# Top-k attention and a gated layer on one core: a layer's rows cast and transposed by DMAs, the sums' constant added by a product, one reduction for row maximum and threshold

## The chip, the cores and the metric

The kernel runs on one core of a Trainium2 chip. The core has five engines with a queue each: TensorE (PE, with its weight loads PEld), VectorE (DVE), ScalarE (ACT), GpSimd (POOL) and SyncE (SP), which here only issues DMAs. An engine works its own queue in order and waits for the others through semaphores. The metric is the device time of one execution in microseconds; before the change it is 821.52 us in the median of three runs.

## The reference

Attention over 8 batches and 8 heads, 576 rows of 64 elements each, in which a row keeps only its 32 largest scores, and behind it a gated (highway) layer of 512 columns over all 4608 rows.

```python
scores = scale * np.matmul(q, k.transpose(0, 1, 3, 2))
kth = np.partition(scores, -top_k, axis=-1)[..., -top_k:-top_k + 1]
mask = scores >= kth
scores = np.where(mask, scores, -1000000000.0)
scores = scores - np.max(scores, axis=-1, keepdims=True)
attn = np.exp(scores)
attn = attn / (np.sum(attn, axis=-1, keepdims=True) + 1e-09)
out = np.matmul(attn, v)
# the heads side by side are x, 4608 x 512
H = np.maximum(x @ w_h, 0.0)
T = 1.0 / (1.0 + np.exp(-(x @ w_t + b_t)))
return T * H + (1.0 - T) * x
```

## The kernel before

The work is cut into units of 128 query rows of one head. A batch has 576 = 4 x 128 + 64 rows, so it has 32 full units, and four units more that each hold the last 64 rows of two heads. Two units make a pair, 18 pairs make a batch, 144 pairs the whole. The main loop, `step(i)`, runs once for every pair, and is a software pipeline: in step i the pair i+2 gets its scores, pair i+1 its threshold, pair i its exponentials and counts, pair i-1 its masks, and pair i-3 its product with v. The order of the instructions on each engine is the order in which `step` writes them (`tc.manual_schedule`); nothing is reordered later.

**One pair's way.** `scores` multiplies q and k in fp32 on TensorE into a PSUM tile of three banks (L293, L302; L310 and L319 for the short units). On VectorE twelve `max` instructions take the eight largest of each sixth of a row (`segments`, L337, into `cand`). `refine` (L342 to L368) merges these lists and ends in a threshold that stands for about the 24th largest score: the list `mid` (L363), and its maximum, written to `wall[:, u, 0]` (L367). `row_max` (L372) reduces the first column of `cand` to the row's maximum in `tk`. `biases` (L375) multiplies both on GpSimd into the biases that ScalarE uses.

ScalarE copies the scores to SBUF (`copy_scores`, L332), then marks and counts the scores above the threshold with a sign pass (`mask_count`, L381). TensorE adds those marks to the PSUM tile (`mask_add`, L394), so that the marked scores sink, and VectorE's `below` (L404) takes the eight largest of what is left. From the count, `hits`, `pick_a` and `pick_b` (L410, L420, L423) choose the exact 32nd value. ScalarE computes the exponentials (`expo`, L400) and a step (`above`, L427), or GpSimd computes the step (`above_one`, L438). VectorE multiplies the exponentials by it (`keep_min`, `keep_mul`, L434, L444), a DMA transposes the product on SP's queue (`transposes`, L465), and `values` (L478) multiplies it with v on TensorE: five products per head accumulate into one PSUM bank, 65 columns each. The 65th column of the v tile `vb` is a constant, 1.0, so that this column of the result is the row's sum.

**The layer.** When a block of 128 rows has all its heads, ScalarE copies the bank to SBUF (`xs_copy`, L492), and `norm` (L538) takes over: VectorE adds 1e-9 to the sum and doubles it (L541), inverts it (L542), and GpSimd multiplies the rows by it (L547). Three pieces follow, one for each step: `xt` transposes the fp32 rows on TensorE (L560) and ScalarE copies them to bf16 (L564); `hh` and `tt` are the two projections (`project`, L506) with their ReLU and tanh on ScalarE (L575, L597). The pieces wait in `ready`, then `layers`, and `late` holds the copy that belongs to the piece of the step before. The sums behind them run on GpSimd and as an accumulating DMA (L658).

**Fillers.** `spare` (L262) issues products whose result nobody reads, on columns of the value bank that are otherwise free: 8 in each step, and 4 more if the step has a layer piece, or 10 more if it has none. The next batch's k and q are loaded by SP, v by GpSimd (`loads_v`, L174, one DMA per head), and `prep_filler` transposes k and q on TensorE (L239), one piece in a step, from the step `k_in` = 6 of a batch on.

Of the kernel before, what the change touches and what calls it, by code (L numbers as in the profile page):

```python
# [10 lines left out]
ALU = mybir.AluOpType  # L11
FP32 = mybir.dt.float32
# [5 lines left out]
J = 4  # L18
# [8 lines left out]
def kernel(  # L27
# [69 lines left out]

    wall = consts.tile([P, NU, NPK], FP32)
    fac = consts.tile([P, 4], FP32)
    nc.vector.memset(fac[:, 0:2], -scale)  # L100
    nc.vector.memset(fac[:, 2:4], -BIGK * (1.0 - 2.0**-24))
    tk = consts.tile([P, NG + 1, 4], FP32)
    be = consts.tile([P, NG + 1, 4], FP32)
    NE = 4
# [5 lines left out]
    csum = consts.tile([P, NU], FP32)  # L110
    nc.vector.memset(tk[:, 0, 2:4], 0.0)
    nc.vector.memset(tk[:, NG, 0:2], 0.0)

    def top(u):
        return tk[:, u // 2, u % 2 : u % 2 + 1]

    def kth(u):
        return tk[:, u // 2 + 1, 2 + u % 2 : 3 + u % 2]

    def tb(u):  # L120
        return be[:, u // 2, u % 2 : u % 2 + 1]

    def eb(u):
        return be[:, u // 2 + 1, 2 + u % 2 : 3 + u % 2]

    NM = 4
    masks = []
# [44 lines left out]
    def loads_v(b, vb):  # L172
        def head(h):
            nc.gpsimd.dma_start(  # L174
                vb[:, h, 0:J, 0:D],
                v[b, h, 0 : J * P, :].rearrange("(p j) d -> p j d", j=J),
            )
# [6 lines left out]
        return [partial(head, h) for h in range(H)] + [partial(ends, o) for o in (0, P2)]  # L184

# [156 lines left out]
    def refine(g, cand):  # L342
        u0, u1 = pairs[g][0], pairs[g][1] + 1
        en = ends[g % NE]
        runs = cand[:].rearrange("p s (k t) r -> p (s k) t r", t=2)
        one, two = runs[:, :, 0, :], runs[:, :, 1, ::-1]
# [3 lines left out]
        mid = cpool.tile([P, 2, 8], FP32, name="mid")  # L350
        nc.vector.tensor_tensor(high[:].rearrange("p (k r) -> p k r", r=8), one, two, ALU.max)  # L351
        yield
        nc.vector.tensor_tensor(low[:].rearrange("p (k r) -> p k r", r=8), one, two, ALU.min)
# [12 lines left out]
        yield  # L366
        nc.vector.tensor_reduce(wall[:, u0:u1, 0], mid[:], mybir.AxisListType.X, ALU.max)  # L367
        yield  # L368


    def row_max(g):
        nc.vector.tensor_reduce(tk[:, g, 0:2], st[g]["cand"][:, :, :, 0], mybir.AxisListType.X, ALU.max)  # L372

    def biases(g):
        return nc.gpsimd.tensor_tensor(be[:, g, :], tk[:, g, :], fac[:], ALU.mult)  # L375

    def mask_count(u, ps):
        m1 = masks[u % NM]  # L380
        nc.scalar.activation(  # L381
            m1[:].bitcast(I8)[:, 1 : 2 * S : 2],
            ps,
            AF.Sign,
            bias=wall[:, u, 0:1],
            scale=ABOVE,
            accum_out=csum[:, u : u + 1],
        )
        return m1
# [13 lines left out]
    def below(u, ps):  # L403
        nc.vector.max(wall[:, u, 1:NPK], ps)  # L404

# [12 lines left out]
    def pick_a(pair, hit):  # L418
        u0, u1 = pair[0], pair[1] + 1
        nc.gpsimd.tensor_tensor(hit[:], hit[:], wall[:, u0:u1, :], ALU.mult)  # L420

    def pick_b(pair, hit):
        nc.vector.tensor_reduce(tk[:, pair[0] // 2 + 1, 2:4], hit[:], mybir.AxisListType.X, ALU.add)  # L423

# [108 lines left out]
    def ffn_pieces(b, qt, xs):  # L533
# [4 lines left out]
        def norm():  # L538
            xs3 = xs[:, 0 : nh * DE].rearrange("p (h e) -> p h e", e=DE)
            rinv = cpool.tile([P, H], FP32, name="rinv")  # L540
            nc.vector.tensor_scalar(rinv[:, 0:nh], xs3[:, :, D], 1e-9, 2.0, ALU.add, ALU.mult)  # L541
# [62 lines left out]
    def blk_norm(k):  # L604
# [3 lines left out]
        rinv = cpool.tile([P, H], FP32, name="rinv")  # L608
        nc.vector.tensor_scalar(rinv[:, 0:nh], xs3[:, :, D], 1e-9, 2.0, ALU.add, ALU.mult)
        nc.vector.reciprocal(rinv[:, 0:nh], rinv[:, 0:nh])  # L610
        nc.vector.tensor_tensor(
# [32 lines left out]

    adds, stores = [], []

# [40 lines left out]
    def start_scores(g):  # L687
# [5 lines left out]
        st[g]["seg"] = 0  # L693
        st[g]["cand"] = cpool.tile([P, 2, NSEG, 8], FP32, name="cand")

# [42 lines left out]
    def step(i):  # L738
# [7 lines left out]
        if live and b + 1 < B:  # L746
# [15 lines left out]
        if prev:  # L762
            pu, ps_ = pairs[i - 1], st[i - 1]
            ps_["r"] = [above(pu[0], ps_["sc"][0])]
            ps_["r"].append(above_one(pu[1], ps_["sc"][1]) if len(pool_work) < (3 if last_steps else 5) else None)
        if late:
            late.pop(0)()
# [25 lines left out]
        ra = refine(i + 1, st[i + 1]["cand"]) if nxt else iter(())  # L793
        for _ in range(2):
            next(ra, None)
        if live:
            hit = hits(pr)
            pick_a(pr, hit)
        added = bool(adds)
        if adds:  # L800
            do_add(i)
        elif todo_v:
# [12 lines left out]
        for _ in ra:  # L815
            pass
        last = None
        for s in range(2):
            if prev:
                u = pu[s]  # L820
                if ps_["r"][s] is not None:
                    ep, last = (keep_min, keep_mul)[s](u, ps_["e"][s], ps_["r"][s])
                else:
                    ep, last = keep(u, ps_["sc"][s], ps_["e"][s])
                ps_["et"][s] = transposes(ep)
        if live:
# [3 lines left out]
        if nxt:  # L830
            masks_of(i + 1)
        while stores and stores[0][0] <= i:
            stores.pop(0)[1]()
# [3 lines left out]
    def begin():  # L837
# [22 lines left out]
        for _ in refine(0, st[0]["cand"]):  # L860
            pass
        row_max(0)
        biases(0)
# [18 lines left out]
    def sure(j, src, scale):  # L882

        nc.scalar.activation(
            signs[:].rearrange("p (g t) -> p g t", t=2),
            src,
# [6 lines left out]
    def finish():  # L893
# [51 lines left out]
        old["et"][0] = transposes(ep)  # L945
        nc.vector.tensor_tensor(hit[:], hit[:], wall[:, pr[0] : pr[1] + 1, :], ALU.mult)
        pick_b(pr, hit)
# [3 lines left out]
        for s, home in enumerate((bank(x2, 1), bank(x1, 0))):  # L951
# [4 lines left out]
            nc.scalar.copy(cur["et"][s][:].rearrange("p c q -> p (c q)"), turned)  # L956
        sure(0, tk[:, 1 : NG + 1, 2:4], 1.0)
        sure(1, tk[:, 0:NG, 0:2], -1.0)
        values_of(i - 1, 0)
# [5 lines left out]
        do_work(nc.vector, NG * dm)  # L965
        nc.vector.scalar_tensor_tensor(cond[:], wall[:, :, 1], ABOVE, wall[:, :, 0], ALU.mult, ALU.add)
        while stores:
            stores.pop(0)[1]()
        sure(2, cond[:].rearrange("p (g t) -> p g t", t=2), 1.0)
        blk_norm(yb)  # L970
# [117 lines left out]
```

## Time and profile before

| | |
|---|---|
| median of three runs | 821.52 us (821.15 to 821.84) |
| the profiled execution | 822.81 us |
| its span, first to last instruction | 821.2 us |
| mean granted TensorE clock | 0.996 |
| one batch of 18 steps, steady | 98.6 us |
| DMA data moved | 91.61 MB |

The profile's page gives each engine's busy time and its share of the span; the chain of work that ended last, followed back from the last instruction; the groups of instructions by source line, with number, busy time, mean duration of one in ns and the idle time of the engine ahead of them; and the DMA queues. The waits are listed by who waited for whom, with the total in us, the number of times and the longest. The windows give the busy time of each engine in a stretch of the span, and the timeline the instructions in order, as start, duration, engine, line. Instructions on one engine overlap: the next can start before the one in front has ended, so the distance of two starts is what an instruction costs its engine, and its duration is longer.

### The profile page before, as it was taken

What the parts mean: (1) busy time and instruction counts of PE and PEld (TensorE: products, weight loads), DVE (VectorE), ACT (ScalarE), POOL (GpSimd) and SP (SyncE); (2) the same over time, 40 slices, a digit from 0 to 9 for tenths busy, and PEclk for the clock granted to TensorE, in tenths of its full rate; (3) what the DMA queues carried; (4) which work ended last, traced back from release to release, by engine and by line L of the source; (5) the groups of instructions that cost most, each with busy time, mean ns of one, the idle gap of its engine ahead of it and who ended that gap; (6) DMA issues with size and microseconds to landing.
All of it is one profiled execution on the core that took longest, in us unless ns stands there. A gap on an engine that the chain in (4) does not pass through costs nothing.

```text
span 821.2 us, 21236 instructions
## 1 busy us (share of the span) xinstructions
PE 714.2 (87%) x6687; PEld 517.6 (63%) x6687; DVE 784.9 (96%) x4162; ACT 772.7 (94%) x1438; POOL 556.1 (68%) x703
## 2 busy tenths in 40 slices
PE   7888988898889988889898898888988898888884
PEld 5666666666666666666666666666666666666552
DVE  6999999999999999999999999999999999999985
ACT  5999999999999999999999999999999999999983
POOL 2666777776677776777667776777667767666550
PEclk9999999999999999999999999999999999999998
DMA  6698878885568655775567765777556865444462
GB/s 120 84 137 140 109 105 129 140 118 84 107 126 142 108 91 110 131 137 108 83 121 132 137 104 72 133 139 131 92 94 129 142 113 97 92 88 72 103 90 74
DMA packets 323145, 91.61 MB, mean 112 GB/s; under 512 B 312144, under 2 KB 315216, under 8 KB 323024
## 3 DMA queue, kind: packets, MB, share of 16 engines
q1 hardware_dynamic: 272688, 74.76, 46.3%
q0 software_dynamic: 48656, 14.95, 18.5%
q8 instruction: 55, 0.90, 0.5%
q10 hardware_dynamic: 1680, 0.46, 0.3%
q14 instruction: 66, 0.54, 0.2%
HBM read 31.72 MB, written 9.44 MB: 50 GB/s over the span
## 4 chain that ended last, share of the span: by engine, by line
DVE 43%; ACT 39%; PE 13%; issue 2%; DMA 1%; SPq 0%; DVEq 0%; ACTq 0%
DVE cand L337 16%; DVE wall L404 12%; ACT m L381 11%; ACT e L400 8%; ACT sc L332 7%; ACT r L427 5%; PE xs L310 4%; PE pso L262 3%; DVE ep L434 3%; DVE ep L444 2%; ACT kT L240 2%; PE xs L293 1%; ACT xs L492 1%; ACT qT L240 1%; DVE en L358 1%
## 5 line engine op out<-in xcount | busy, mean ns | idle before, releaser
L337 DVE MAX8 cand<-xs 128x8 f32<-128x96 f32 x1728 | 297.4, 249 | 13.9 <-PE xs L319 9.4
L262 PE MATMUL pso<-cst,ident_b 128*128 128x252 bf16 x1935 | 256.5, 272 | 38.8 <-ACT xs L492 36.7
L438 POOL TENSOR_SCALAR ro<-sc,tk 128x576 bf16<-128x576 f32 x136 | 234.8, 1726 | 0.0
L262 PEld LDWEIGHTS <-ident_b 128*128 128x128 bf16 x1935 | 183.4, 98 | 77.8 <-issue 45.9
L400 ACT ACTIVATE e<-sc,be 128x576 bf16<-128x576 f32 x288 | 228.6, 794 | 0.0
L404 DVE MAX8 wall<-xs 128x8 f32<-128x576 f32 x288 | 204.3, 751 | 4.2 <-PE xs L394 3.6
L293 PE MATMUL xs<-kT,qT 64*128 64x256 f32 x1024 | 145.6, 400 | 35.2 <-DVE high L351 28.8
L332 ACT COPY sc<-xs 128x1152 f32<-128x1152 f32 x144 | 162.1, 1126 | 1.5 <-DVE cand L337 1.3
L293 PEld LDWEIGHTS xs<-kT,qT 64*128 64x128 f32 x1024 | 93.6, 186 | 64.7 <-issue 32.4
L381 ACT ACTIVATE m<-xs,wall 128x576 int8<-128x576 f32 x144 | 108.5, 754 | 13.1 <-DVE wall L367 10.7
L420 POOL TENSOR_TENSOR hit<-hit,wall 128x18 f32<-128x18 f32 x143 | 32.1, 225 | 128.4 <-DVE hit L410 119.1
L394 PE MATMUL xs<-m,ident_b 128*128 128x512 bf16 (+1 forms) x576 | 104.2, 285 | 11.9 <-ACT m L381 9.2
L381 ACT ACTIVATE m<-sc,wall 128x576 int8<-128x576 f32 x144 | 113.0, 784 | 0.0
L427 ACT ACTIVATE r<-sc,be 128x576 bf16<-128x576 f32 x143 | 111.4, 779 | 0.0
L375 POOL TENSOR_TENSOR be<-tk,fac 128x4 f32<-128x4 f32 x144 | 28.9, 201 | 93.4 <-DVE ep L444 51.8
L478 PEld LDWEIGHTS <-et 128*128 128x128 bf16 (+1 forms) x1600 | 68.6, 100 | 21.0 <-issue 3.5
L478 PE MATMUL pso<-vb,et 128*128 128x65 bf16 (+1 forms) x1600 | 74.6, 194 | 1.7 <-DMA et<-ep 1.6
L394 PEld LDWEIGHTS <-ident_b 128*128 128x128 bf16 x576 | 50.7, 97 | 39.7 <-issue 18.3
L302 PEld LDWEIGHTS xs<-kd,qT 128*128 128x128 f32 x256 | 38.1, 188 | 42.5 <-issue 42.1
L434 DVE TENSOR_TENSOR ep<-e,r 128x576 bf16<-128x576 bf16 x143 | 64.6, 452 | 0.1
L302 PE MATMUL xs<-kd,qT 128*128 128x128 f32 x256 | 62.5, 326 | 0.0
L444 DVE TENSOR_TENSOR ep<-e,ro 128x576 bf16<-128x576 bf16 x136 | 61.4, 452 | 0.0
(130 smaller groups left out, 1107.7 us busy)
## 6 DMA issues: line engine op xcount, KB each, us to landing
kin<-in_k_dram SPq DMA_DIRECT2D x64, 128.0 KB, 2.9
qin<-in_q_dram SPq DMA_DIRECT2D x62, 128.0 KB, 3.0
out_dram<-s SPq DMA_DIRECT2D x30, 256.0 KB, 2.5
s<-h POOLq DMA_DIRECT2D x29, 256.0 KB, 4.1
vb<-in_v_dram POOLq DMA_DIRECT2D x80, 64.0 KB, 3.2
et<-ep SPq DMA_TRANSPOSE x286, 2.7
kin<-in_k_dram SPq DMA_DIRECT2D x16, 64.0 KB, 2.4
qin<-in_q_dram SPq DMA_DIRECT2D x14, 64.0 KB, 2.5
```

Source lines behind the costliest of these rows:

```text
L262: nc.tensor.matmul(po["t"][:, 4 * DE : BANK], ident_b[:], cst[:, 0 : BANK - 4 * DE], start=True, stop=True, skip_group_check=True,)
L293: nc.tensor.matmul(ps[:, mo + n0 : mo + n0 + 256], qT[r : r + D, hp, qs : qs + P], kT[r : r + D, hp, n0 : n0 + 256], start=(n0 == 0), stop ...
L302: nc.tensor.matmul(ends, qT[:, hp, qs : qs + P], kd[:, hp, :], start=True, stop=True)
L332: nc.scalar.copy(sc[:], both)
L337: nc.vector.max(cand[:, s, :], sc[:, s * SEG : (s + 1) * SEG])
L381: nc.scalar.activation(m1[:].bitcast(I8)[:, 1 : 2 * S : 2], ps, AF.Sign, bias=wall[:, u, 0:1], scale=ABOVE, accum_out=csum[:, u : u + 1],)
L394: nc.tensor.matmul(ps[:, s0:s1], ident_b[:], m1[:, s0:s1], start=False, stop=True, skip_group_check=True)
L400: nc.scalar.activation(e[:], sc, AF.Exp, bias=tb(u), scale=scale)
L404: nc.vector.max(wall[:, u, 1:NPK], ps)
L427: nc.scalar.activation(r[:], sc, AF.Relu, bias=eb(u), scale=BIGK)
L438: nc.gpsimd.tensor_scalar(r[:], sc, kth(u), None, ALU.is_ge)
L478: nc.tensor.matmul(pso[r0 : r0 + ql, col : col + DE], ets[s][:, c, gi * P2 : gi * P2 + ql], vb[:, h, vc, :], start=(c == 0), stop=(c == nc ...
```

## The change

- `column` loads v for batches 1 to 7 in four DMAs, each with a quarter of the rows of all eight heads, in place of eight DMAs of one head each.
- The constant column of `vb` is 2.0, and `values` opens each head's chain with one more product: a row of ones (1 x 128, or 1 x 64) by a row `tiny` that is zero except for 2e-9 in its last column, both fp32. The bank's last column is then twice the sum, plus 2e-9, and `norm` and `blk_norm` only invert it.
- `refine` writes its list `mid` into the second column of `cand` (which now has eight lists in place of six, two of them padded with -3e38), and one reduction takes the maximum of the first and the second column, that is, the row maximum and the threshold, into neighbouring columns of `wall`. `row_max` and `tk` are gone; `wall` holds their values.
- The first of the two masks (`masked(0)`) is issued between the writing of the list and that reduction; `pick_b` moves in front of the list.
- For 37 of the 40 blocks, `cast` (a DMA from GpSimd's queue, fp32 to bf16, SBUF to SBUF) and two steps later `turn` (a transposing DMA on SP's queue) take the place of `xt`. Casts are issued where no accumulating DMA is due in the step, ahead of the loads of v.
- Preparation of the next batch starts at `k_in` = 4 in place of 6. It is skipped in a step that has a layer's copy waiting, unless it would come late, and a layer piece is issued during the preparation only in a step that prepares.

```diff
-        nc.gpsimd.memset(vb[:, :, :, D:DE], 1.0)
+        nc.gpsimd.memset(vb[:, :, :, D:DE], 2.0)
+    tiny = consts.tile([1, DE], FP32)
+    nc.vector.memset(tiny[:], 0.0)
+    nc.vector.memset(tiny[:, D:DE], 2.0e-9)
+    row1 = consts.tile([1, P], FP32)
+    nc.vector.memset(row1[:], 1.0)
...
+        def column(j):
+            nc.gpsimd.dma_start(
+                vb[:, :, j, 0:D],
+                v[b, :, 0 : J * P, :].rearrange("h (p j) d -> p h j d", j=J)[:, :, j, :],
+            )
+        mains = [partial(column, j) for j in range(J)] if b else [partial(head, h) for h in range(H)]
...
         nc.vector.scalar_tensor_tensor(
-            out=mid[:], in0=en[:, 1, :, 0:8], scalar=-1.0, in1=en[:, 0, :, 0:8], op0=ALU.mult, op1=ALU.min
+            out=cand[:, :, :, 1], in0=en[:, 1, :, 0:8], scalar=-1.0, in1=en[:, 0, :, 0:8], op0=ALU.mult, op1=ALU.min
         )
         yield
-        nc.vector.tensor_reduce(wall[:, u0:u1, 0], mid[:], mybir.AxisListType.X, ALU.max)
+        nc.vector.tensor_reduce(
+            wall[:, u0:u1, TOP : THR + 1],
+            cand[:, :, :, 0:2].rearrange("p s r k -> p s k r"),
+            mybir.AxisListType.X,
+            ALU.max,
+        )
-    def row_max(g):
-        nc.vector.tensor_reduce(tk[:, g, 0:2], st[g]["cand"][:, :, :, 0], mybir.AxisListType.X, ALU.max)
...
             for gi, h in enumerate(heads):
+                nc.tensor.matmul(
+                    pso[r0 : r0 + ql, col : col + DE], row1[:, 0:ql], tiny[:], start=True, stop=False
+                )
                 for c in range(nck):
...
-                        start=(c == 0),
+                        start=False,
...
-            nc.vector.tensor_scalar(rinv[:, 0:nh], xs3[:, :, D], 1e-9, 2.0, ALU.add, ALU.mult)
-            nc.vector.reciprocal(rinv[:, 0:nh], rinv[:, 0:nh])
+            nc.vector.reciprocal(rinv[:, 0:nh], xs3[:, :, D])
...
-                ready.extend([xt, hh, tt])
+                if by_dma:
+                    casts.append(cast)
+                else:
+                    ready.extend([xt, hh, tt])
+        by_dma = isinstance(b, int) and units[-1][0:2] > (b, qt + 2)
+        def cast():
+            xb = xpool.tile([P, dm], BF16, name="xb")
+            nc.gpsimd.dma_start(xb[:, 0:w], st["x"][:, 0:w])
+            return partial(turn, xb)
+        def turn(xb):
+            st["xT"] = fpool.tile([P, n_g, P], BF16, name="xT")
+            nc.sync.dma_start_transpose(st["xT"][:, 0:ng, :], xb[:, 0:w])
+            ready.extend([hh, tt])
...
-            if k_in == (6 if b else 7):
+            if k_in == (4 if b else 7):
...
-        ev = prep_filler()
+        ev = None if busy and i > SPB and len(to_prep) < 16 - k_in else prep_filler()
...
-        if layers:
+        if layers and (not to_prep or ev or last_steps):
             late.append(layers.pop(0)())
...
-        if nxt:
-            row_max(i + 1)
-        next(ra, None)
         if live:
             pick_b(pr, hit)
+        next(ra, None)
+        masked(0)
         for _ in ra:
             pass
+        last = masked(1)
```

More of the change, by code (lines that the diff above doesn't have):

```diff
@@ L96 @@
         nc.vector.memset(pidx[:, jj : jj + 1], S - 2.0 * (TOP_K - jj))
[L98 to L103, printed above, removed]
+    TOP, THR, KTH = 0, 1, NPK + 1
+    wall = consts.tile([P, NU + 2, NPK + 2], FP32)
+    fac = consts.tile([P, 2, 2], FP32)
+    nc.vector.memset(fac[:, :, 0], -scale)
+    nc.vector.memset(fac[:, :, 1], -BIGK * (1.0 - 2.0**-24))
+    be = consts.tile([P, NG + 1, 2, 2], FP32)
     NE = 4
@@ L110 @@
     csum = consts.tile([P, NU], FP32)
[L111 to L115, printed above, removed]
+    nc.vector.memset(wall[:, 0:2, KTH : KTH + 1], 0.0)
     def kth(u):
-        return tk[:, u // 2 + 1, 2 + u % 2 : 3 + u % 2]
+        return wall[:, u + 2, KTH : KTH + 1]
     def tb(u):
-        return be[:, u // 2, u % 2 : u % 2 + 1]
+        return be[:, u // 2, u % 2, 0:1]
     def eb(u):
-        return be[:, u // 2 + 1, 2 + u % 2 : 3 + u % 2]
+        return be[:, u // 2 + 1, u % 2, 1:2]
+    cands = []
+    for i in range(4):
+        cand = consts.tile([P, 2, 8, 8], FP32, name=f"cand{i}")
+        nc.vector.memset(cand[:, :, NSEG:, 0:1], -3.0e38)
+        cands.append(cand)
     NM = 4
@@ L344, in refine @@
         en = ends[g % NE]
-        runs = cand[:].rearrange("p s (k t) r -> p (s k) t r", t=2)
-        one, two = runs[:, :, 0, :], runs[:, :, 1, ::-1]
+        one = cand[:, :, 0:NSEG:2, :]
+        two = cand[:, :, 1:NSEG:2, ::-1]
         high = cpool.tile([P, 2 * HALF], FP32, name="high")
@@ L643, in blk_out @@
         return k["b"], k["qt"], o
-    adds, stores = [], []
+    adds, stores, casts, turns = [], [], [], []
     def do_work(engine, width):
@@ L765, in step @@
             ps_["r"].append(above_one(pu[1], ps_["sc"][1]) if len(pool_work) < (3 if last_steps else 5) else None)
+        busy = bool(late)
         if late:
@@ L793, in step, with masked @@
         ra = refine(i + 1, st[i + 1]["cand"]) if nxt else iter(())
+        def masked(s):
+            if not prev:
+                return None
+            u = pu[s]
+            if ps_["r"][s] is not None:
+                ep, ins = (keep_min, keep_mul)[s](u, ps_["e"][s], ps_["r"][s])
+            else:
+                ep, ins = keep(u, ps_["sc"][s], ps_["e"][s])
+            ps_["et"][s] = transposes(ep)
+            return ins
         for _ in range(2):
@@ L798, in step @@
             pick_a(pr, hit)
-        added = bool(adds)
+        added = bool(adds or casts)
         if adds:
             do_add(i)
+        elif casts:
+            turns.append((i + 2, casts.pop(0)()))
         elif todo_v:
@@ L831, in step @@
             masks_of(i + 1)
+        while turns and turns[0][0] <= i:
+            turns.pop(0)[1]()
         while stores and stores[0][0] <= i:
@@ L861, in begin @@
             pass
-        row_max(0)
         biases(0)
```

43 lines of the change are left out of this document (16 added, 27 removed).

## The prediction

> **What bounds the kernel now.** I read the page's busy times and its chain first, then the waits, then one steady batch (18 steps) in the windows, then the timeline of two steps.
>
> ```profile
> span 821.2 us, 21236 instructions
> PE 714.2 (87%) x6687; PEld 517.6 (63%) x6687; DVE 784.9 (96%) x4162; ACT 772.7 (94%) x1438; POOL 556.1 (68%) x703
> DVE 43%; ACT 39%; PE 13%; issue 2%; DMA 1%; SPq 0%; DVEq 0%; ACTq 0%
> ...
> 403.09:501.67 98.58, 87.65 (x827) 63.64 (x826) 96.06 (x515) 96.03 (x180) 70.65 (x89) 1.00 0.64 116
> ```
>
> DVE and ACT are both full: of a batch's 98.58 us they work 96.06 and 96.03. PE comes third with 87.65, and the chain already runs through it for 13%. So the reader should not see one bound but three, two at 97% and one at 89%. What PE does with the other 107.0 us (821.2 less 714.2) is in the waits:
>
> ```profile
> PE pso L262 <- ACT xs L492: 36.7, 70, 0.8
> PE xs L293 <- DVE high L351: 28.8, 48, 1.5
> PE xs L394 <- ACT m L381: 9.2, 33, 0.6
> PE xs L310 <- DVE high L351: 6.0, 7, 0.9
> PE xs L293 <- DVE wall L404: 3.7, 16, 0.4
> ```
>
> The first row is no slack. PE finishes the value products, ACT copies the bank, and only then may the filler products (`spare`) write the same bank again; the timeline shows that wait at its shortest:
>
> ```profile
> 409.62 0.48 PE L478 MATMUL pso<-vb,et 128*128 128x65 bf16 x10
> 410.14 0.38 ACT L492 COPY xs<-pso 128x260 f32<-128x260 f32 x1 [0.16 <-PE pso L478]
> 410.57 1.02 PE L262 MATMUL pso<-cst,ident_b 128*128 128x252 bf16 x8 [0.46 <-ACT xs L492]
> ```
>
> ACT starts 0.04 us after the products end (409.62 + 0.48 = 410.10) and PE still loses 0.46. Seventy times 0.46 are 32 us that stay whatever ACT does. The other four rows, 28.8 + 9.2 + 6.0 + 3.7 = 47.7 us, are PE's real slack. The rest of its idle time, 107.0 - 36.7 - 47.7 = 22.6 us, is start, end and small gaps; I keep it.
>
> **The change, part by part.** *The sums' constant on TensorE.* Before each head's chain of value products a new one-row fp32 product opens the group: 8 batches x 8 heads x 4 full query tiles = 256 with 128 columns of weights, and 64 with 64 columns for the short tile, 320 in all. The trace has no one-row product. I build its price from the nearest fp32 product and from what it costs to change the array's shape:
>
> ```profile
> 407.73 0.30 PEld L302 LDWEIGHTS xs<-kd,qT 128*128 128x128 f32 x2 [0.33 <-issue]
> 407.74 0.49 PE L302 MATMUL xs<-kd,qT 128*128 128x128 f32 x2
> 408.06 1.24 PE L262 MATMUL pso<-cst,ident_b 128*128 128x252 bf16 x10
> ...
> 403.69 0.38 PE L508 MATMUL fp<-bt,cst 128*128 128x512 bf16 x1
> 403.90 0.59 PE L262 MATMUL pso<-cst,ident_b 128*128 128x252 bf16 x4
> ...
> 809.17 0.38 PE L508 MATMUL xs<-bt,cst 128*128 128x512 bf16 x1
> 809.48 0.64 PE L516 MATMUL xs<-wh,xT 128*64 128x256 bf16 x8
> ...
> 810.51 0.27 PE L520 MATMUL fp<-bt,cst 128*64 128x256 bf16 x1
> 810.72 0.29 PE L980 MATMUL pso<-ones,cnt 128*1 128x1 f32 x6
> ...
> L302 PEld LDWEIGHTS xs<-kd,qT 128*128 128x128 f32 x256 | 38.1, 188 | 42.5 <-issue 42.1 <-DVE kd L252 0.4
> L293 PEld LDWEIGHTS xs<-kT,qT 64*128 64x128 f32 x1024 | 93.6, 186 | 64.7 <-issue 32.4 <-PE fp L239 12.2 <-DVE wall L404 9.3
> ```
>
> One fp32 product of the program is two records, each with its weight load (L302 is issued once a step and shows x2). It holds PE from 407.74 to 408.06, 0.32 us: a load, a second load beside the first stream, the second stream. The two loads together take 0.30 at 188 ns each, so the second starts 0.11 after the first; three pieces of 0.11 make the 0.32. With 65 columns to stream instead of 128 the last piece is 0.11 x 65/128 = 0.05: 0.27 us. For the 64-column weights the loads halve: 0.05 + 0.06 + 0.05 = 0.16.
>
> A change of shape: the same L508 product is followed after 0.21 us by a product of its own shape (403.69 to 403.90) and after 0.31 by one of 128*64 (809.17 to 809.48): 0.10 us. From 128*64 to 128*1 the next starts 0.21 after L520, whose 256 columns take about 0.11 by the filler's pace ((1.24 - 0.27)/9 for 252): 0.10 again, so a one-column operand gets a shape of its own and I take it that a one-row operand does too. Into that shape and out again are 0.20. Price: 0.47 us x 256 + 0.36 x 64 = 143 us of PE. Lowest: a value product's own pace, below. Highest: 0.52, if the first bf16 load behind it is exposed as well (167 us).
>
> The Trainium skill, "TensorEngine Tiling", Key Properties, says the same of the shape: changing the tiling mode drains TensorE; without a drain the second rival's 857 would stand. The Trainium skill, "TensorE: Matmul & The Clock Gate", LDWEIGHTS, has a load's time go by its columns and not its rows, an estimate of 0.107 us for 128; the 64-row and 128-row loads above (186 and 188 ns) bear that out, and no run here shows one row. Were one-row loads free, the product would cost 0.11 + 0.20 = 0.31, 99 us instead of 143, and the result 876.
>
> In exchange VectorE's add-and-scale goes, 38 x 165 ns = 6 us, and 2 more in the tail.
>
> *The layer's rows by DMA.* 37 of 40 blocks lose their transposes on PE and their cast on ACT. The blocks' pieces in the step loop fall from three to two, and a step without a piece runs 10 fillers instead of 4:
>
> ```profile
> L262 PE MATMUL pso<-cst,ident_b 128*128 128x252 bf16 x1935 | 256.5, 272 | 38.8 <-ACT xs L492 36.7 <-POOL ident_b masks.py:199 1.8 <-ACT qT L240 0.2
> L560 PE MATMUL fp<-ident_f,x 128*128 128x128 f32 x134 | 21.0, 275 | 0.0
> L564 ACT CAST xT<-fp 128x512 bf16<-128x512 f32 (+1 forms) x37 | 20.4, 552 | 0.0
> L541 DVE TENSOR_SCALAR rinv<-xs 128x8 f32<-128x8 f32 (+1 forms) x38 | 6.3, 165 | 0.0
> L372 DVE TENSOR_REDUCE tk<-cand 128x2 f32<-128x12 f32 x144 | 22.3, 155 | 0.0
> L423 DVE TENSOR_REDUCE tk<-hit 128x2 f32<-128x18 f32 x144 | 23.8, 165 | 0.0
> L478 PE MATMUL pso<-vb,et 128*128 128x65 bf16 (+1 forms) x1600 | 74.6, 194 | 1.7 <-DMA et<-ep 1.6
> L658 POOL DMA_DIRECT2D s<-h x36 | 33.3, 925 | 8.2 <-POOL hit L420 8.2
> L174 POOL DMA_DIRECT2D vb<-in_v_dram x64 | 53.0, 828 | 7.8 <-issue 6.8 <-PE fp L239 0.9
> et<-ep SPq DMA_TRANSPOSE x286, 2.7
> ```
>
> ACT loses 20.4 us. PE loses 21.0 and gains 37 x 6 fillers x 0.133 (256.5/1935) = 29.4: +8.4. POOL issues 37 casts, by the nearest row 0.93 each (34 us), and saves four of a batch's ten loads of v in seven batches, 28 x 0.83 = 23 us less whatever longer lists the four wide ones need; POOL has 30% free and what waits behind the cast there (`biases`) waits for the masks anyhow. SP takes 37 more transposes; they are queued behind the two of the step and land about 2.7 us after issue, while the product that reads them comes in the next step behind the scores, so I cost them at nothing; if they land late, PE stands, at some 1 us x 37 at most.
>
> *One reduction for maximum and threshold.* 144 reductions of 155 ns go, but the remaining one reads 32 values a row instead of 16. L372 and L423 differ by 10 ns for 6 values, so +27 ns: 22.3 - 3.9 = 18.4 us off DVE. The mask in front of it (0.37 us to the next) less the reduction gone (0.12) makes the threshold 0.25 us later, and ACT's first sign pass waits for it:
>
> ```profile
> 407.52 0.17 DVE L367 TENSOR_REDUCE wall<-mid 128x2 f32<-128x16 f32 x1
> 407.61 0.45 DVE L434 TENSOR_TENSOR ep<-e,r 128x576 bf16<-128x576 bf16 x1
> 407.73 0.74 ACT L381 ACTIVATE m<-xs,wall 128x576 int8<-128x576 f32 x1
> 407.98 0.45 DVE L444 TENSOR_TENSOR ep<-e,ro 128x576 bf16<-128x576 bf16 x1
> ```
>
> ACT starts 0.04 us after the threshold here, so nothing hides this today. Behind a later PE it is hidden: the signs are needed only when PE comes to add them.
>
> *Which preparation runs when.* The new conditions keep a layer piece and a preparation out of the same step. That evens out ACT and moves no work off PE.
>
> **The sum.** DVE falls to about 784.9 - 18.4 - 6.3 = 760 and ACT to 752, so by these two alone the time would fall by some 19 us. But PE rises to 714.2 + 143 + 8.4 = 866 busy, and its 32 us behind the copy and 22.6 us of start, end and gaps stay: 920 us of span, the slack of 47.7 used up. As a check by batch: 87.65 + 32 x 0.47 + 8 x 0.36 + 8.4/8 + 9 x 0.46 = 110.8 against 98.58, times eight plus the 32.6 outside the eight batches, 919. The profiled run took 822.8, 1.6 more than its span and 1.3 more than the median of 821.52, so 920 of span answers to about 920 in the median. I predict 920: PE becomes the bound, and what DVE and ACT are spared turns into their waiting.
>
> **The rivals.** *The product is cheap (faster).* If it costs what a value product does, 74.6/1600 = 0.047 us, it adds 15 us; PE then needs 714.2 + 15 + 8.4 + 55 = 793, DVE and ACT stay the bound, and 821.2 - 19 = 802 results (785 if the even steps also recover waits). It decides below 0.08 us each, where PE's sum meets 802; from 0.14 on PE's sum passes 821. The L302 rows speak against it. The Trainium skill, "TensorEngine Tiling", Instruction Overhead, speaks for it: about 60 cycles for any short product, by my estimate 0.03 us each and PE at 787. But it counts neither loads nor drains, and both show in the trace.
>
> *No change of shape.* If the one-row product keeps the full shape, 256 x 0.27 + 64 x 0.16 = 79 us: 714.2 + 79 + 8.4 + 55 = 857. Against it stands the 0.10 at L980.
>
> *The later threshold binds.* If PE stays out of it, 0.25 x 144 = 36 us of waiting ACT against the 19 saved: 838. For it speak the 0.04 us above; against it that ACT stands for the threshold in few steps now and has less to do:
>
> ```profile
> ACT m L381 <- DVE wall L367: 10.7, 26, 0.7
> ```
>
> **How the numbers follow.** Forecast (shape changes and loads both paid, 876 to 948): 0.62. Full shape kept (830 to 876): 0.16. Later threshold (815 to 840): 0.06. Cheap product (785 to 815): 0.14. The offsets that cancel within 0.2%: 0.02. A measurement here tells 0.2% from nothing (the runs lie within 0.7 us). Faster 0.14, same 0.03, slower 0.83. The range takes in the first two and half of the third, 832 to 948; the forecast's own is 876 to 948, its upper end the 0.52 us (24 us more) with 4 us of waits that persist.
>
> **What would show it.** Right: a group of one-row products with 640 records, PE busy near 866 us, steps of about 6.15 us instead of 5.48, DVE near 760 and ACT near 752 us busy with new waits for PE at the scores, PE's waits for DVE gone. Wrong: PE's time per value chain up by less than 0.14 us a head; or PE idle for DMA-landed rows; or ACT idle behind the threshold. The prediction fails first if a one-row product neither drains the array nor shows its loads.

## The result, and the profile after

The changed kernel takes 914.09 us in the median (911.32 to 915.3) against 821.35 us before (821.15 to 821.84): 1.1123 times the time, 95% interval 1.1095 to 1.1151. The profiled execution took 913.2 us, its span is 911.5.

The page of the changed kernel: span, busy times, and the shares of the chain that ended last. Behind them, from the windows, a stretch of 110 us, about one batch: its length, then the busy time of PE, PEld, DVE, ACT and POOL, PE's clock, the DMA share and GB/s.

```profile
span 911.5 us, 22548 instructions
PE 859.4 (94%) x7415; PEld 615.2 (67%) x7415; DVE 776.4 (85%) x3984; ACT 762.3 (84%) x1401; POOL 559.9 (61%) x712
PE 87%; ACT 8%; DVE 2%; issue 1%; DMA 1%; SPq 0%; ACTq 0%; DVEq 0%
```

```profile
350.00:460.00 110.00, 105.40 (x919) 75.73 (x918) 94.92 (x492) 94.62 (x175) 71.70 (x90) 1.00 0.71 114
```

Before, DVE and ACT carried 82% of the chain; now PE carries 87% of it. In this stretch PE works 105.40 of 110.00 us, while DVE and ACT, which had 2.5 us of rest in a batch, now have 15. (Batches 2 to 7 take 110.0 to 111.8 us each, 6.16 us a step.) The waits say the same from the other side (who waited <- for whom: total us, times, longest):

```profile
DVE cand L350 <- PE xs L315: 90.4, 112, 3.2
ACT xs L508 <- PE pso L494: 83.3, 72, 2.9
PE pso L275 <- ACT xs L508: 32.5, 70, 0.5
PE xs L407 <- ACT m L394: 3.2, 11, 0.6
PE xs L306 <- DVE high L363: 0.8, 1, 0.8
```

PE's own waits for DVE and ACT have gone from 47.7 us to a few; what stays is the wait for the copy of the bank (L508). In their place DVE stands 90.4 us for the scores and ACT 83.3 us for the value products. The groups of the new and the changed lines (mean ns of one behind the busy time):

```profile
L489 PE MATMUL pso<-tiny,row 1*128 1x65 f32 (+1 forms) x640 | 131.1, 284 | 0.0
L379 DVE TENSOR_REDUCE wall<-cand 128x4 f32<-128x32 f32 x144 | 29.4, 204 | 0.1
L579 POOL DMA_DIRECT2D xb<-x x37 | 23.0, 623 | 10.9 <-POOL hit L433 10.9
```

and, among the DMA issues, the transposed rows (us from issue to landing):

```profile
xT<-xb SPq DMA_TRANSPOSE x37, 2.5
```

The product is there as 640 records of a shape of its own, 1*128. The timeline of PE shows two heads of a step (start, duration, and so on):

```profile
454.13 0.65 PE L407 MATMUL xs<-m,ident_b 128*128 128x512 bf16 x4
454.71 0.43 PE L489 MATMUL pso<-tiny,row 1*128 1x65 f32 x2
455.08 0.33 PE L494 MATMUL pso<-vb,et 128*128 128x65 bf16 x5
455.34 0.43 PE L489 MATMUL pso<-tiny,row 1*128 1x65 f32 x2
455.70 0.33 PE L494 MATMUL pso<-vb,et 128*128 128x65 bf16 x5
```

From one head to the next are 455.34 - 454.71 = 0.63 us. Without the product, value products start 0.032 us apart, 0.16 a head. The product costs 0.47 us a head.

### The profile page after: what moved, and what is told of

The parts are those of the page before. It is cut to its first block, busy times and chain, and to the rows that moved or that the text cites. A ratio compares the mean times of both kernels' runs of the same rounds, so it can differ in the third digit from the quotient of the medians.

```text
span 911.5 us, 22548 instructions
## 1 busy us (share of the span) xinstructions
PE 859.4 (94%) x7415; PEld 615.2 (67%) x7415; DVE 776.4 (85%) x3984; ACT 762.3 (84%) x1401; POOL 559.9 (61%) x712
## 4 chain that ended last, share of the span: by engine, by line
PE 87%; ACT 8%; DVE 2%; issue 1%; DMA 1%; SPq 0%; ACTq 0%; DVEq 0%
PE pso L275 25%; PE xs L306 14%; PE pso L489 12%; PE pso L494 9%; PE xs L407 8%; PE fp L522 5%; PE xs L315 5%; PE xs L323 3%; ACT xs L508 3%; PE fp L252 3%; ACT m L394 2%; ACT e L413 1%; PE fp L532 1%; DVE cand L350 1%; PE fp L524 1%
## 5 line engine op out<-in xcount | busy, mean ns | idle before, releaser
L350 DVE MAX8 cand<-xs 128x8 f32<-128x96 f32 x1728 | 298.9, 249 | 112.8 <-PE xs L315 90.4
L275 PE MATMUL pso<-cst,ident_b 128*128 128x252 bf16 x2157 | 282.4, 273 | 34.6 <-ACT xs L508 32.5
L275 PEld LDWEIGHTS <-ident_b 128*128 128x128 bf16 x2157 | 205.2, 98 | 76.9 <-issue 41.6
L451 POOL TENSOR_SCALAR ro<-sc,wall 128x576 bf16<-128x576 f32 x136 | 234.5, 1725 | 0.0
L413 ACT ACTIVATE e<-sc,be 128x576 bf16<-128x576 f32 x288 | 225.0, 782 | 0.0
L306 PE MATMUL xs<-kT,qT 64*128 64x256 f32 x1024 | 148.5, 408 | 2.3 <-ACT qT L253 1.5
L489 PE MATMUL pso<-tiny,row 1*128 1x65 f32 (+1 forms) x640 | 131.1, 284 | 0.0
L489 PEld LDWEIGHTS pso<-tiny,row 1*128 1x128 f32 (+1 forms) x640 | 86.7, 172 | 43.1 <-issue 34.0
L494 PE MATMUL pso<-vb,et 128*128 128x65 bf16 (+1 forms) x1600 | 107.1, 197 | 0.0
L508 ACT COPY xs<-pso 128x260 f32<-128x260 f32 x72 | 27.1, 376 | 83.3 <-PE pso L494 83.3
L388 POOL TENSOR_TENSOR be<-wall,fac 128x4 f32<-128x4 f32 x144 | 28.8, 200 | 71.8 <-DVE ep L457 54.3
L407 PEld LDWEIGHTS <-ident_b 128*128 128x128 bf16 x576 | 50.1, 98 | 29.1 <-issue 5.4
```

Of the source, the lines that this page charges most:

```text
L275: nc.tensor.matmul(po["t"][:, 4 * DE : BANK], ident_b[:], cst[:, 0 : BANK - 4 * DE], start=True, stop=True, skip_group_check=True,)
L306: nc.tensor.matmul(ps[:, mo + n0 : mo + n0 + 256], qT[r : r + D, hp, qs : qs + P], kT[r : r + D, hp, n0 : n0 + 256], start=(n0 == 0), stop ...
L350: nc.vector.max(cand[:, s, :], sc[:, s * SEG : (s + 1) * SEG])
L407: nc.tensor.matmul(ps[:, s0:s1], ident_b[:], m1[:, s0:s1], start=False, stop=True, skip_group_check=True)
L413: nc.scalar.activation(e[:], sc, AF.Exp, bias=tb(u), scale=scale)
L451: nc.gpsimd.tensor_scalar(r[:], sc, kth(u), None, ALU.is_ge)
```

## The experiments

A step's length below is the distance from the first `max` of one step (L350) to that of the next. "Half clock" are the stretches in which the trace's clock record stands at 0.5.

### Is it the product?

First the changed kernel without the product (and so without the 2e-9 in the sums; the same holds for all later kernels "without the product"), then the kernel before with nothing but the product added.

```diff
-                nc.tensor.matmul(
-                    pso[r0 : r0 + ql, col : col + DE], row1[:, 0:ql], tiny[:], start=True, stop=False
-                )
...
-                        start=False,
+                        start=(c == 0),
```

> The changed kernel without the one-row product: the value chain opens its own group, the column stays 2.0, and the 2e-9 is left out of the sums. Theory (the product makes PE the bound): PE busy falls by about 135 us to some 725, DVE and ACT are the bound again and keep what the other parts save, so 785 to 806 us, point 800. Rival (the later threshold or the rows by DMA cost the time): it stays above 838 us, with ACT waiting for the threshold or PE for the rows. Rival (the product is cheap and something else on PE grew): PE busy stays above 800 us.

Measured: 818.23 us, ratio 0.9966 (0.9956 to 0.9976).

```profile
PE 721.9 (88%) x6679; PEld 527.2 (64%) x6775; DVE 770.1 (94%) x3984; ACT 759.9 (93%) x1401; POOL 559.7 (68%) x712
ACT 40%; DVE 25%; PE 25%; DMA 4%; issue 3%; POOL 1%; SPq 1%; ACTq 0%; DVEq 0%; POOLq 0%
```

The product costs 914.1 - 818.2 = 96 us, and PE 859.4 - 721.9 = 137 us. But the rest of the change saves only 3 us where 19 were expected; that is followed up below.

The other way round, in the kernel before:

```diff
-        nc.gpsimd.memset(vb[:, :, :, D:DE], 1.0)
+        nc.gpsimd.memset(vb[:, :, :, D:DE], 2.0)
...
+                nc.tensor.matmul(
+                    pso[r0 : r0 + ql, col : col + DE], row1[:, 0:ql], tiny[:], start=True, stop=False
+                )
...
-            nc.vector.tensor_scalar(rinv[:, 0:nh], xs3[:, :, D], 1e-9, 2.0, ALU.add, ALU.mult)
-            nc.vector.reciprocal(rinv[:, 0:nh], rinv[:, 0:nh])
+            nc.vector.reciprocal(rinv[:, 0:nh], xs3[:, :, D])
```

> The kernel before with the one-row fp32 product alone (and the column of 2.0, without VectorE's add-and-scale). Theory: 320 products of 0.36 to 0.47 us, 143 us of PE; its waits for DVE and ACT vanish, so 714 + 143 + 55 = 912 us, 900 to 920. Rival (other parts of the change cost the time): 815 to 830 us.

Measured: 918.3 us, 1.1183 (1.1161 to 1.1205), PE busy 846.5 us. The product alone makes the whole loss; the rest of the change gives some 4 us of it back.

### What the 0.47 us consist of

Three kernels give the same product another shape or type: all 128 rows in fp32 (each adds 2e-9/128), all 128 rows in bf16, and one row in bf16.

```diff
-    tiny = consts.tile([1, DE], FP32)
+    tiny = consts.tile([P, DE], FP32)
...
-    nc.vector.memset(tiny[:, D:DE], 2.0e-9)
-    row1 = consts.tile([1, P], FP32)
+    nc.vector.memset(tiny[:, D:DE], 2.0e-9 / P)
+    row1 = consts.tile([P, P], FP32)
```

> The changed kernel, the product still fp32 but over all 128 rows (ones of 128x128 by 2e-9/128 in each row), so that the array keeps its shape. Theory (0.20 of the 0.47 us are the two changes of shape): 320 x 0.20 = 64 us less than the changed kernel, 850 us (835 to 865). Rival (the cost lies in fp32 loads and two streams alone): 905 to 915 us. Rival (the shape is all of it): about 800 us.

Measured: 844.69 us, 1.0286 (1.0266 to 1.0307).

```diff
-    tiny = consts.tile([1, DE], FP32)
+    tiny = consts.tile([P, DE], BF16)
...
-    nc.vector.memset(tiny[:, D:DE], 2.0e-9)
-    row1 = consts.tile([1, P], FP32)
-    nc.vector.memset(row1[:], 1.0)
+    nc.vector.memset(tiny[:, D:DE], 4.0e-9)
+    row1 = cst
```

> The changed kernel with the product in bf16 over all 128 rows (the existing constant matrix by 4e-9): same shape and type as the value products beside it. Theory: it costs what a value product costs, 0.03 to 0.05 us, 10 to 15 us of PE in all; PE is no longer the bound and the time is that of the kernel without the product within 3 us, about 802 us. Rival (an opening product costs by itself, whatever its shape and type): 840 us or more.

Measured: 818.71 us, 0.9964 (0.995 to 0.9979), the same as with no product.

```diff
-    tiny = consts.tile([1, DE], FP32)
+    tiny = consts.tile([1, DE], BF16)
...
-    row1 = consts.tile([1, P], FP32)
+    row1 = consts.tile([1, P], BF16)
```

> The one-row product in bf16 instead of fp32: the shape still changes, but there is one record and one load in place of two each. Full shape costs 844.7 - 818.7 = 26 us more in fp32 than in bf16. If loads and shape add up (0.27 + 0.20), the same 26 us go here: 914 - 26 = 888, range 880 to 895, and PE's L489 loses about half of its records' time. If the change of shape hides behind the loads of the fp32 product or the reverse, another number comes out: under 870 the shape's part is smaller with one record, over 900 the second record cost nothing next to the drain.

Measured: 853.2 us, 1.0383 (1.0362 to 1.0404), 35 us under what adding the two parts gave. The 26 us in that sum were too few: in full bf16 PE is no longer the fullest engine (729.6 us busy, DVE 770.2, ACT 759.4), so making it cheaper still could not show in the time. By PE's busy time, fp32 costs 859.4 - 781.0 = 78 us over one row and 774.8 - 729.6 = 45 over all rows. PE's timelines of the three, in the order full fp32, full bf16, row bf16, two heads each:

```profile
461.07 0.33 PE L489 MATMUL pso<-tiny,row 128*128 128x65 f32 x2
...
461.40 0.41 PE L489 MATMUL pso<-tiny,row 128*128 128x65 f32 x2
461.65 0.32 PE L494 MATMUL pso<-vb,et 128*128 128x65 bf16 x5
461.81 0.38 PE L275 MATMUL pso<-cst,ident_b 128*128 128x252 bf16 x2
```

```profile
461.08 0.19 PE L488 MATMUL pso<-tiny,cst 128*128 128x65 bf16 x1
...
461.27 0.19 PE L488 MATMUL pso<-tiny,cst 128*128 128x65 bf16 x1
```

```profile
459.90 0.20 PE L489 MATMUL pso<-tiny,row 1*128 1x65 bf16 x1
...
460.30 0.20 PE L489 MATMUL pso<-tiny,row 1*128 1x65 bf16 x1
```

| one head, start to start | full 128 rows | one row |
|---|---|---|
| no product | 0.16 | |
| bf16 | 0.19 (+0.03) | 0.40 (+0.24) |
| fp32, first head | 0.33 (+0.17) | 0.63 (+0.47) |
| fp32, second head | 0.41 (+0.25) | |

The first three rows are the distance from a step's first product to its second; the last is the distance from the second product to the filler behind its chain (461.40 to 461.81). In bf16 over all rows both heads take 0.19 us. In the one-row kernels the distance between the two products holds the way out of the shape and into it again, so it is a whole price.

The change of shape by itself is 0.24 - 0.03 = 0.21 us. The second record and the slower loads of fp32 are 0.17 - 0.03 = 0.14 in the first head and 0.25 - 0.03 = 0.22 in the second of the full shape, and 0.63 - 0.40 = 0.23 in the one-row shape. The loads show where the difference comes from. On PEld, of the full fp32 kernel (both heads) and then of the changed kernel:

```profile
460.86 0.40 PEld L489 LDWEIGHTS pso<-tiny,row 128*128 128x128 f32 x2
...
461.37 0.30 PEld L489 LDWEIGHTS pso<-tiny,row 128*128 128x128 f32 x2
```

```profile
454.71 0.29 PEld L489 LDWEIGHTS pso<-tiny,row 1*128 1x128 f32 x2 [0.24 <-issue]
```

In the full shape the first head's load starts at 460.86, 0.21 us ahead of its product (461.07), beside the products in front; the second head's starts only 0.03 ahead (461.37 against 461.40). In the one-row shape the load starts with its product (454.71 both) after 0.24 us of standing, and in the one-row bf16 kernel too (459.90 both). So an fp32 load that runs ahead adds 0.14 us, and one that does not adds 0.22 to 0.23, in either shape; shape and type then add up, 0.03 + 0.21 + 0.22 = 0.46 of the 0.47. That a load of the new shape does not run beside products of the old one is read off these rows; no run changed it by itself.

The time follows PE's price only above a floor. With PE at 721.9 (no product) and 729.6 us (full bf16) the time stays at 818; at 774.8 (full fp32) it is 845, at 781.0 (row bf16) 853, and at 859.4 it is 914. So the two-way table cannot add up in the time.

### Does only the amount of PE's work count?

If it does, fewer fillers must give the time back. First the changed kernel with the fillers cut to a few, then to about half:

```diff
-        spare(8)
+        spare(2)
...
-        spare(4 if late else 10)
+        spare(2 if late else 4)
```

> The changed kernel, product and all, with 2 fillers a step in place of 8 and 2 or 4 in place of 4 or 10. Nothing but work without a reader is taken from PE: about 176 products a batch, 150 us in all. Theory (PE is the bound, by its own work in order): the 914 us fall by most of that until DVE and ACT bind, 805 to 830 us, unless PE's granted clock falls. Rival (the one-row products delay the value chain and so ACT's copy, as a latency and not as work): little changes, 890 us or more.

Measured: 905.45 us, 1.1017 (1.0995 to 1.1039). What was expected from PE's work alone is missed by far, and the rival's 890 us or more is what came. PE has 1420 records fewer (7415 to 5995), at the fillers' pace of 0.13 us some 190 us of work, yet its busy time falls by 72 us and the time by 9. Part of that is the pace: in the kernels without the product further below, a filler taken out frees only (721.9 - 642.1)/900 = 0.09 us. The page's busy times, and two windows that show why (length, busy time of PE, PEld, DVE, ACT and POOL, the clock); then the timeline in the first window:

```profile
PE 787.3 (87%) x5995; PEld 514.5 (57%) x5995; DVE 778.3 (86%) x3984; ACT 761.4 (84%) x1401; POOL 558.6 (62%) x712
```

```profile
44.90:62.00 17.10, 16.42 (x80) 10.91 (x80) 12.61 (x69) 11.36 (x21) 8.94 (x14) 0.50 0.69 109
62.00:72.20 10.20, 8.53 (x74) 5.77 (x72) 8.92 (x45) 9.12 (x18) 4.22 (x5) 1.00 1.01 145
```

```profile
49.78 0.69 PE L489 MATMUL pso<-tiny,row 1*128 1x65 f32 x2
...
50.79 0.69 PE L489 MATMUL pso<-tiny,row 1*128 1x65 f32 x2
```

In 30 stretches, 148 us in all, the granted clock stands at half, mostly for 3.4 us, and a head takes 1.01 us instead of 0.63; the changed kernel has 4 such stretches, 17 us. The 46 steps touched by one take 6.69 us on average, the others 5.69 (their median is 5.76). So with the product in place the fillers hold the clock up: the mean is 0.992 with all of them and 0.919 here. The Trainium skill, "TensorE: Matmul & The Clock Gate", Part 1, has the clock go to half in windows of about 3.4 us, and the trace agrees on both; but its rule against PE gaps longer than that ("HAM oscillation — how this bites in real kernels") does not cover this case, since PE's longest wait here is 1.8 us:

```profile
PE xs L407 <- ACT m L394: 56.3, 135, 0.8
...
PE xs L306 <- DVE high L363: 9.9, 25, 1.8
```

Even the undisturbed steps of 5.69 us make 144 x 5.69 + 33 = 852 us, not 805 to 830. PE now stands 56.3 us for ACT's signs. To part this from the clock, the milder cut:

```diff
-        spare(8)
+        spare(4)
...
-        spare(4 if late else 10)
+        spare(2 if late else 6)
```

> The changed kernel, product in place, with 4 fillers a step instead of 8, and 2 or 6 behind them instead of 4 or 10. In the kernel without the product the same cut took PE from 721.9 to 642.1 us and left the clock at 0.995, so here PE should work about 859.4 - 80 = 780 us at an undisturbed clock. Theory (only the amount of PE's work decides): 780 and the 52 us that PE stands in the changed kernel (911.5 - 859.4) make 832, range 822 to 842. Rival (the products also lengthen the way from mask_add to the next scores, so that steps do not get shorter than the 5.76 us which the cut to 2 fillers showed at full clock): 144 x 5.76 + 33 = 862, range 852 to 872. If the clock falls again (mean under 0.97), 870 to 905.

Measured: 882.02 us, 1.0734 (1.0712 to 1.0755), clock 0.976. PE is at 775.9 us as the theory had it, but the time is 50 us above its 832. It is also 10 above the rival's upper end: 16 steps that touch a stretch at half clock take 6.56 us instead of 5.78, 16 x 0.78 = 12 us; without that it would be 870, inside the rival's range. What parts 870 from 832 is a wait of PE that is 38.6 us longer than in the changed kernel (3.2):

```profile
PE xs L407 <- ACT m L394: 41.8, 124, 0.6
```

The amount of PE's work is refuted as the only cause. The full fp32 kernel, with as much work on PE (774.8) and all fillers, takes 845.

Why ACT's signs come late shows in the chain that ended last, here of the kernel with 4 fillers, in order of time (start, length, what), through parts of two steps, from a sign pass on:

```profile
400.23 1.60 ACT m L394 x4
...
401.87 0.19 PE xs L407
...
402.21 0.43 PE pso L489 x2
402.64 0.27 PE pso L494 x5
402.90 0.36 PE pso L489 x2
403.26 0.27 PE pso L494 x5
403.53 0.43 PE pso L275 x4
...
408.91 0.38 ACT xs L508
409.29 0.68 ACT e L413
409.96 1.01 ACT sc L345
```

and of the kernel without the product and with the same fillers (next section), one whole step:

```profile
399.58 1.59 ACT m L394 x4
...
401.21 0.41 PE xs L407 x2
401.62 0.33 PE pso L491 x10
...
401.97 0.38 ACT xs L505
402.35 0.67 ACT e L413
403.02 1.01 ACT sc L345
404.03 0.67 ACT e L413
...
404.72 1.60 ACT m L394 x4
```

This second chain is a closed loop: signs on ACT, `mask_add` and the value products on PE, the copy of the bank on ACT, the other ACT work, and the next signs 404.72 - 399.58 = 5.14 us later, of which only 0.08 is nobody's work. The product stands in the middle of this loop, between `mask_add` and the copy: 402.21 to 403.53, 1.32 us for two heads instead of 0.33. In the two steps shown PE then works on to 408.89 almost without a break, so PE's own work and ACT's signs take turns in setting the step. The reading is that the product costs PE's throughput and, where PE has room again, the way through PE. It is read off these chains: no run moved the product out of the loop with PE's work unchanged. Nor is the loop every step's: in the whole run without the product and with 4 fillers ACT has 49% of the chain, DVE 23% and PE 18%.

### Where the 19 us of the rest went

Three kernels without the product, each with one other part undone: the first mask behind the reduction, the old rules of preparation and layer pieces, no rows by DMA.

```diff
-        masked(0)
         for _ in ra:
             pass
+        masked(0)
```

> The kernel without the product, with the first mask behind the common reduction again, so that the threshold is 0.37 us earlier. Theory B (the later threshold eats the gain): 800 to 808 us. Rival A or C: 816 to 820 us, or more, since the reduction then follows directly on the instruction that writes its list.

Measured: 821.32 us, 0.9996 (0.9985 to 1.0007). The mask in front is worth 3 us in the net; the later threshold does not eat the gain.

```diff
-            if k_in == (4 if b else 7):
+            if k_in == (6 if b else 7):
...
-        ev = None if busy and i > SPB and len(to_prep) < 16 - k_in else prep_filler()
+        ev = prep_filler()
...
-        if layers and (not to_prep or ev or last_steps):
+        if layers:
```

> The kernel without the product, with the old rules for when preparation and layer pieces run (from step 6 on, in every step, layer pieces at once). Steps 12, 14 and 16 of a batch are 0.4 to 0.7 us longer without the product than before, the rest about 0.1 shorter. Theory D (the new rules push preparation into the long steps at the batch's end): 805 to 812 us. Rival: 817 to 825 us.

Measured: 824.18 us, 1.0033 (1.0021 to 1.0046). The new rules are worth 6 us.

```diff
-        by_dma = isinstance(b, int) and units[-1][0:2] > (b, qt + 2)
+        by_dma = False
```

> The kernel without the product (818.2, its sums without the 2e-9), with every block transposed on TensorE and cast by ScalarE again, no row by DMA. ACT gets 20 us of casts back (760 to 780), PE 21 us of transposes, less some 29 us of fillers. If the rows by DMA are worth what they take off ACT, the time is 818 + 8 to 20 = 826 to 838. If the casting and transposing DMAs make up for it by lateness (steps 12, 14 and 16), 814 to 820.

Measured: 815.76 us, 0.9934 (0.9917 to 0.9952): the rows by DMA bring nothing in time, rather a loss of some 2 us.

```profile
PE 710.6 (87%) x6596; PEld 519.7 (64%) x6687; DVE 772.9 (95%) x3984; ACT 772.1 (95%) x1438; POOL 531.8 (65%) x673
```

ACT works 12 us more than without the product (772.1 against 759.9) and PE 11 less (710.6 against 721.9, fewer fillers), and the time falls by 2 us. That is the second expectation, 814 to 820. Why sparing ACT 12 us gained nothing was not separated: with the rows by DMA come 222 more fillers and the waits for the rows, and the chain that ended last has 7% fillers and 4% DMA with them, 3% and 1% without. So the parts are worth +3 and +6 us, and the rows by DMA -2. What is left for the reduction, the add on VectorE and the wide loads of v is about -3 us if the parts add, which no run showed.

If fillers cost time, fewer must help here too, where nothing else on PE is short:

```diff
-        spare(8)
+        spare(4)
...
-        spare(4 if late else 10)
+        spare(2 if late else 6)
```

> The kernel without the product, 4 fillers a step in place of 8 and 2 or 6 in place of 4 or 10 (some 105 us of PE less). Without the product it came out at 818 us where 802 was expected. Theory A (PE is still a bound in single steps, the ones with a preparation and a layer piece, since the rows by DMA add 222 fillers): 795 to 806 us. Rival B (the threshold that comes 0.25 us later eats the gain): no change, 815 to 820 us. Rival C (ACT's and DVE's own unevenness): 810 to 818 us.

Measured: 809.12 us, 0.9845 (0.9829 to 0.9862), clock 0.995. That lies just below the band of 810 to 818. About half of the fillers out bring 9 us, against the 16 that the rest of the change had not brought. The kernel before was not run with fewer fillers, so it is not shown that these 9 us belong to the change. The waits of this kernel still held one that a larger buffer takes away:

```profile
ACT h L602 <- DMA s<-h: 3.7, 3, 2.2
```

```diff
-            h2 = fpool.tile([P, dm], FP32, name="h2")
+            h2 = fpool.tile([P, dm], FP32, name="h2", bufs=3)
```

> The kernel without the product (2e-9 left out of the sums), with 4 fillers a step and 2 or 6 behind them (809.1), and a third buffer for the tile h2, which in step 15 of a batch ScalarE could not write for 0.75 us because the accumulating DMA was still reading it, while PE waited 0.86 us for ScalarE. If that wait was on the path: 8 x 0.8 = 6 us less, 803, range 800 to 806. If another wait takes its place: 807 to 811.

Measured: 805.04 us (804.32 to 809.19), 0.9813 (0.9782 to 0.9843); the wait is gone from the list. It had come in three batches and not in all eight, as the expectation took it: in batches 5 to 7 step 15 took 8.45 (with a stretch at half clock in it), 5.96 and 5.97 us, and takes 5.46, 5.46 and 6.18 now. It is the fastest version of the study, 1.9% under the kernel before. Against the step before it, 4 us in the median, the two intervals still touch.

## Why the prediction came out as it did

It was right in the direction, in the cause and nearly in the size: 914 us against 920, from PE's work (859.4 us against 866) and PE's remaining idle time (911.5 - 859.4 = 52.1 us against 54.6). Point by point:

- **The price of the product**: 0.47 us a head forecast, 0.47 measured; 137 us of PE between the kernels with and without it against 143. The parts hold as well. The shape was 0.20 and is 0.21 us; that a one-row operand is a shape of its own, which had been taken over from a one-column operand, is shown by the 1*128 rows and the two bf16 kernels. The loads and streams were 0.27 from the L302 product and are 0.47 - 0.21 = 0.26 in the one-row shape, where the loads do not run ahead; the prediction had not said that they could, and in the full shape they do (0.17 and 0.25). For the short tile 0.36 was forecast; its heads are 0.53 us apart, 0.37 more than without the product. One sum in it is off: the highest price and the one with free loads were multiplied by all 320 products (167 and 99 us), though 64 of them are short; 0.52 for the full and 0.41 for the short ones make 159. The Trainium skill, "TensorEngine Tiling", Key Properties, has a change of mode drain TensorE; the 0.21 us bear it out. The Trainium skill's Instruction Overhead rule on the same page, which would have made the product cheap, does not hold for this product, though the full bf16 product, at 0.03 us, agrees with it.
- **PE's wait for the copy of the bank**: 32 us taken as fixed, 32.5 measured. The slack of 47.7 us was used up as forecast: `mask_add`'s wait for ACT is 3.2 us, the scores' wait for DVE 0.8.
- **More fillers, fewer transposes**: +8.4 us of PE forecast, 721.9 - 714.2 = 7.7 measured without the product.
- **The steps**: 6.15 us forecast, 6.16 measured over batches 2 to 7.
- **DVE near 760 and ACT near 752**: measured 776.4 and 762.3. This term was mis-sized. It added mean durations, but an instruction overlaps its neighbours' ends, so taking it away can free less than it lasts: the durations of DVE's instructions do fall by 1117.3 - 1093.8 = 23.5 us, about as forecast, but its busy time by 8.5 only, and by 784.9 - 770.1 = 14.8 without the product. The reduction itself is as forecast (204 ns against 171 + 27).
- **DMAs**: the casts cost POOL 0.62 us each instead of 0.93; the transposed rows land after 2.5 us and PE waits for none of them. Without the product PE waits 4.8 us for them.
- **The rival "cheap product"** had 802 us. With the product cheap (full bf16) the time is 819: its 19 us for the rest were 3. The sum took a falling load of DVE and ACT for a falling time; but a step is set by the way through several engines (such as the loop ACT - PE - ACT above), and taking transposes off PE and casts off ACT, with what came in their place, gained nothing (815.8 us with them back).
- **The rival "no change of shape"** had 857; the full fp32 kernel, which is that case, takes 845, because the loads run ahead there (0.17 and 0.25, 0.21 in the mean, instead of 0.27).
- **The rival "later threshold"** had 838. Undoing the order costs 3 us, so it falls.
- What the prediction left out is that the product also lies on the way from the signs to the copy of the bank, and that with it the clock hangs on the fillers. Neither changed the result, because PE was full anyway. They decide what comes of an attempt to make room on PE: 72 to 84 us less work there brought 9 and 32 us.

## What to carry to other kernels

A tiny product is not a tiny cost: look at its shape and its type before its length. The same addition, in the shape and type of its neighbours, costs 0.03 us instead of 0.47 and no measurable time in the whole kernel.

Before work is counted as saved, ask whether it lies in the loop that sets the step. Follow the chain from one instance of an instruction to the next instance of the same one; here one such loop (signs, `mask_add`, value products, copy, exponentials, signs) was 5.14 us. Taking 12 us of work off ACT brought no gain in time, while taking out about half of the fillers and adding a third buffer brought 818.2 - 805.0 = 13 us.

## What had not been expected of the chip

- The load of a product in another array shape did not run ahead in the rows seen (0.24 us of standing on PEld), so that a slow load lies open: fp32 adds 0.23 us there, against 0.14 where its load starts 0.21 us ahead of the product.
- The clock falls with the product in place and fillers cut (30 stretches at half clock, mean 0.919; 11 with the milder cut, mean 0.976), though PE is busy 87 to 88% of the span by its rows. Without the product and with the milder cut, PE is busy 79% and the mean clock is 0.995. Busy time by the trace is therefore not what the clock follows. That one-row products count for little there would fit, but no run tested it, and the one-row bf16 product with all fillers, PE busy 92%, left the mean at 0.996.
